# A second level of Strassen's scheme in the second FFN product, from the second chunk on

## The chip, the cores and the metric

The kernel runs on one core of one Trainium2 chip. The metric is the device time of one execution in microseconds, the median of several runs. Lower is better. The core's engines are TensorE (PE; PEld is its weight load), VectorE (DVE), ScalarE (ACT), GpSimd (POOL) and SyncE (SP, which here only starts DMAs). Each works through its own queue in order, and they wait for one another through semaphores.

## The reference

An attention block whose heads are mixed before and after the softmax feeds a Fourier mixing block with a feed-forward network (FFN). Only the end of it is touched by the change:

```python
    u = x + mixed
    mu = np.mean(u, axis=-1, keepdims=True)
    var = np.mean((u - mu) ** 2, axis=-1, keepdims=True)
    un = (u - mu) / np.sqrt(var + 1e-06)
    ch = np.maximum(un @ w_ch1, 0.0) @ w_ch2
    return (u + ch).astype(np.float32)
```

There are 8 x 448 = 3584 rows of 768 columns, and the hidden width is 3072. All is fp32; the weights arrive as 64-bit floats.

## The kernel before

The first 850 us or so are attention and Fourier mixing. The rest is the FFN, in `ffn_phase`. It cuts the rows into 7 blocks of 512 (`t`) and the hidden width into 6 chunks of 512 (`c`). One **step** `n` is one block times one chunk, 42 steps in all, blocks inside chunks. Each step makes two products, and each of these is done by one level of Strassen's scheme in its Winograd form: instead of eight products of half-size matrices, seven, with sums of the operands ahead and sums of the results behind.

`first(n)` makes the hidden values. Each of its seven parts (loop over `ORDER`) is six matmuls of 128 x 128 weights on 256 columns (L985). Parts accumulate into three PSUM tiles, called P, Q and R. ScalarE copies or VectorE adds what a part ends into the tile `h`, and ScalarE applies the ReLU. At the end VectorE makes the operand sums hs1, hs2 and h11 - h21 (L1020 to L1022).

`second(n, h)` multiplies them with the second weights. Each of its seven parts is four matmuls of 384 columns (L1042): two halves of the rows (`x`), and two blocks of the inner dimension (`kf`) that add up in PSUM. In chunk 0 VectorE adds the results to `u` and SyncE writes them out. In chunks 1 to 5 ScalarE copies them into `od` tiles, VectorE adds to these, and GpSimd starts a DMA that adds the tile to what is in memory (L1062). VectorE makes h12 - hs2 in the middle (L1065).

The weights of the next chunk are made ready alongside. `_Weights` turns the 64-bit numbers into 32-bit ones with seven VectorE instructions for each piece, forms the operand sums of the weights with four more for each slice, and writes them to scratch memory. A slice has four pieces, so 32 VectorE instructions; a chunk has five slices, three of the first weights (pieces 256 wide) and two of the second (384 wide). GpSimd starts the loads of the raw pieces (L213, two pieces ahead) and the writes (L221). `wts.add(c + 1, ...)` queues one slice in each of a chunk's early steps, and `wts.deal(k)` places up to `k` of the queued VectorE instructions at that point of the program: 3 after six of the seven parts of `first` and 4 after every part of `second`, 46 a step.

The order of TensorE's and VectorE's instructions in the FFN is the order of the program. ScalarE's and GpSimd's is left to the scheduler:

```python
    with tc.manual_schedule(engines={ET.PE, ET.DVE}):
```

[...]P, Q and R have two tiles each, and after the first step P and R share two more, so that every third request for P or R takes an extra tile.

## Time and profile before

| what | value |
|---|---|
| median of 3 runs | 2410.84 us (2409.32 to 2411.01) |
| the profiled execution | 2417.4 us, of which span 2415.6 us |
| granted TensorE clock | 0.994 of full speed |
| VectorE, 851 to 1158 us (chunk 0) | 213.73 of 307 us busy |
| VectorE, 1158 to 1195 us (a step with weight conversion) | 19.55 of 37 us busy |
| VectorE, 2152 to 2404 us (the last chunk, none) | 55.29 of 252 us busy |
| GpSimd in the same three | 62.25, 11.24, 32.73 us |
| output DMA, issue to landing | 6.3 us |
| raw weight load, issue to landing | 3.7 us |

A page line of a group gives the source line, the engine, the operation, what is written from what, the shapes and the number of instructions; then the busy time and the mean duration in ns; then the idle time ahead of them and what ended it. A timeline line gives start, length, engine, line, operation and, behind x, how many instructions of the kind were merged. An fp32 matmul shows as two instructions. Matmuls overlap in the pipeline, so one's duration is longer than the distance between two.

### The profile page before, as it was taken

The page shows a single profiled execution, that of the slowest core. Times are in us where ns is not written, and L with a number is a line of the kernel's source. Part 1 is how long each engine was busy: PE and PEld are TensorE (multiplying, and loading weights), DVE is VectorE, ACT ScalarE, POOL GpSimd, SP SyncE. Part 2 cuts the span into 40 slices and gives each one's busy share as a digit, 9 for nine tenths or more (in the row PEclk, how much of TensorE's full clock was granted, in tenths as well). Part 3 has the DMA queues.
Part 4 walks back from the last instruction along what each step waited for, and adds up shares of the span by engine and source line. Part 5 has one row for each costly group of instructions (what it writes and reads, how often), then busy time and mean ns, then how long its engine had stood idle before and what let it go on. Part 6 is the DMA issues. An engine that isn't in the chain of part 4 may idle for free.

```text
span 2415.6 us, 55276 instructions
## 1 busy us (share of the span) xinstructions
PE 2363.0 (98%) x21680; PEld 1592.6 (66%) x21680; DVE 1408.6 (58%) x2859; ACT 932.7 (39%) x2335; POOL 960.3 (40%) x1395
## 2 busy tenths in 40 slices
PE   6999999999999999999999999999999999999998
PEld 2555555555555577677777777777777777777775
DVE  3888888888887767775555255624552455421221
ACT  4777777666667532231222222222222222222221
POOL 3587877868776541210223023212222223111111
PEclk9999999999999999999999999999999999999999
DMA  7565555655554565658687677777686777585453
GB/s 160 163 179 167 183 172 166 190 162 180 169 164 157 165 248 184 213 180 308 165 198 187 182 201 171 197 184 201 173 205 149 221 190 188 137 232 112 108 115 53
DMA packets 207184, 427.59 MB, mean 177 GB/s; under 512 B 38990, under 2 KB 128870, under 8 KB 206926
## 3 DMA queue, kind: packets, MB, share of 16 engines
q1 hardware_dynamic: 129902, 261.60, 32.4%
q0 software_dynamic: 71456, 161.08, 31.1%
q8 instruction: 173, 2.83, 0.5%
q10 hardware_dynamic: 5568, 1.38, 0.4%
q14 instruction: 85, 0.70, 0.1%
HBM read 211.98 MB, written 129.39 MB: 141 GB/s over the span
## 4 chain that ended last, share of the span: by engine, by line
PE 77%; issue 11%; DMA 4%; DVE 2%; POOL 2%; ACT 1%; SPq 1%; POOLq 0%; ACTq 0%; DVEq 0%
PE psP L985 15%; PE psP L1042 14%; PE psR L985 7%; PE psR L1042 7%; PE mx L486 6%; PE ms L459 5%; PE ms L547 5%; PE po L520 5%; PE psQ L1042 4%; PE psQ L985 4%; DMA Kr<-Sb 3%; POOL out_dram L1062 2%; PE ms L661 2%; PE ms L434 1%; SPq L475 1%
## 5 line engine op out<-in xcount | busy, mean ns | idle before, releaser
L985 PE MATMUL psP<-ub,w1t 128*128 128x256 f32 x2016 | 462.5, 379 | 0.0
L1042 PE MATMUL psP<-w2t,h 128*128 128x384 f32 x1344 | 460.9, 486 | 0.0
L985 PEld LDWEIGHTS psP<-ub,w1t 128*128 128x128 f32 x2016 | 382.8, 190 | 60.7
L1062 POOL DMA_DIRECT2D out_dram<-od x140 | 170.9, 1221 | 590.5 <-DVE od L1060 467.7
L1042 PEld LDWEIGHTS psP<-w2t,h 128*128 128x128 f32 x1344 | 254.4, 190 | 165.9
L510 POOL TENSOR_SCALAR PP<-PP,rcp 128x448 f32<-128x448 f32 x384 | 253.8, 670 | 230.0 <-DVE rcp L508 201.2
L500 ACT ACTIVATE PP<-mx,nmx 128x448 f32<-128x448 f32 x384 | 240.7, 632 | 174.4 <-DVE nmx L493 162.9
L493 DVE TENSOR_REDUCE nmx<-mx 128x1 f32<-128x448 f32 x384 | 223.0, 617 | 94.4 <-PE mx L486 92.5
L213 POOL DMA_DIRECT2D raw<-in_moe_w_ch_dram x120 | 72.6, 605 | 515.1 <-DVE tmp L257 507.7
L1058 ACT COPY od<-psP 128x384 f32<-128x384 f32 x210 | 100.6, 479 | 437.1 <-PE psP L1042 437.1
L486 PE MATMUL mx<-Kr,kw 60*32 60x448 f32 x3072 | 236.4, 552 | 17.2 <-DMA Kr<-Sb 13.7
L996 DVE TENSOR_TENSOR h<-h,psQ 128x512 f32<-128x512 f32 x42 | 28.9, 687 | 381.3 <-PE psQ L985 381.3
L985 PE MATMUL psR<-ub,w1t 128*128 128x256 f32 x1008 | 231.3, 379 | 0.0
L1042 PE MATMUL psR<-w2t,h 128*128 128x384 f32 x672 | 230.5, 486 | 0.0
L531 DVE STREAM_TRANSPOSE Pv<-po 128x896 f32<-128x896 f32 x192 | 212.6, 1107 | 9.0 <-PE po L520 6.1
L520 PE MATMUL po<-PP,kw 60*32 60x448 f32 x3072 | 214.2, 543 | 3.4 <-POOL PP L510 1.8
L459 PE MATMUL ms<-kT,qT 64*32 64x448 f32 (+1 forms) x3072 | 207.2, 547 | 7.3 <-ACT qT L330 6.4
L985 PEld LDWEIGHTS psR<-ub,w1t 128*128 128x128 f32 x1008 | 191.4, 190 | 25.9
L330 ACT COPY Sb<-ms 124x448 f32<-124x448 f32 x384 | 184.0, 542 | 36.7 <-DMA Kr<-Sb 16.1
L547 PEld LDWEIGHTS ms<-Pv,vv 64*64 64x64 f32 x5376 | 144.5, 133 | 70.5 <-issue 37.3
L1042 PEld LDWEIGHTS psR<-w2t,h 128*128 128x128 f32 x672 | 127.2, 190 | 87.4
L547 PE MATMUL ms<-Pv,vv 64*64 64x120 f32 x5376 | 167.8, 269 | 1.0 <-issue 1.0
(101 smaller groups left out, 2925.0 us busy)
## 6 DMA issues: line engine op xcount, KB each, us to landing
ub<-ub SPq DMA_DIRECT2D x294, 384.0 KB
Kr<-Sb SPq DMA_DIRECT2D x768, 105.0 KB
out_dram<-od POOLq DMA_DIRECT2D x140, 384.0 KB, 6.3
raw<-in_moe_w_ch_dram POOLq DMA_DIRECT2D x72, 256.0 KB, 3.8
raw<-in_moe_w_ch_dram POOLq DMA_DIRECT2D x48, 384.0 KB, 3.7
w<-wst POOLq DMA_DIRECT2D x126, 128.0 KB, 3.5
w<-wst POOLq DMA_DIRECT2D x84, 192.0 KB, 3.5
w1t<-w SPq DMA_DIRECT2D x42, 384.0 KB
```

Of the source, the lines that this page charges most:

```text
L330: (nc.scalar.copy if eng == "a" else nc.vector.tensor_copy)(out=out, in_=in_)
L459: nc.tensor.matmul(pss[x][o:o + hi - lo, :S], st["qT", xx][64 * x:64 * x + 64, y, lo:hi], st["kT", xx][64 * x:64 * x + 64, y, :], start=Tr ...
L486: nc.tensor.matmul(mx[x][64 * z + o:64 * z + o + 32, :S], kw1[64 * x:64 * x + KR, o:o + 32], Kr[64 * x:64 * x + KR, z, :], start=True, sto ...
L493: nc.vector.tensor_reduce(nmx[:, :], steps[T]["mx"][x][:, :S], axis=AX.X, op=ALU.max, negate=True)
L500: nc.scalar.activation(steps[T]["PP"][:, x, :], steps[T]["mx"][x][:, :S], ACTF.Exp, bias=steps[T]["nmx", x][:, :], accum_out=steps[T]["den ...
L510: nc.gpsimd.tensor_scalar(PP[:, x, :], PP[:, x, :], rcp[:, x:x + 1], 1.0, op0=ALU.mult, op1=ALU.mult)
L520: nc.tensor.matmul(po[o:o + 32, z, :S], kw2[64 * z:64 * z + KR, y, :], PP[64 * z:64 * z + KR, :, c * HS:(c + 1) * HS], start=True, stop=True)
L531: nc.vector.transpose(g["Pv"][:, T % GT, :].rearrange("p (z s) -> p z s", z=2), steps[T]["po"][:, :, :S])
L547: nc.tensor.matmul(pss[y][64 * x:64 * x + 64, :nu * R], st["v", pr][64 * y:64 * y + 64, x, jb * D:(jb + 1) * D], _ap(Pv, 64 * y * rp + 32 ...
L985: nc.tensor.matmul(p[:, m, :], w1[i][:, kc, m * P:(m + 1) * P], ub[:, kc, :], start=i in OPENS and m == kc == 0, stop=kc == NK - 1, skip_g ...
L1042: nc.tensor.matmul(p, lhs[i][:, kf, x * P:(x + 1) * P], w2[i][:, kf, :], start=i in OPENS and kf == 0, stop=kf == FM - 1, skip_group_check ...
L1062: nc.gpsimd.dma_start(out=acc[t, r, d], in_=os[r, d][:, :, :], accum_op=ALU.add)
```

## The change

From chunk 1 on, each of the seven half-size products of the second product is made by the scheme once more. Its left operand is 256 rows by 256, its right one 256 by 384; so it becomes seven products of quarter size, each one matmul of 128 x 128 weights on 192 columns: 49 matmuls of 192 columns a step in place of 28 of 384.

The new operand sums are: `quarter`, four sums for each of the seven left operands, grouped (h11 and h22 on GpSimd, h21, hs1 and hs2 on VectorE, h12 and h12 - hs2 on GpSimd, 12 instructions in all a step); and `halves`, four sums for each of the seven right operands, on GpSimd, in the first step of each chunk (28 instructions). `second2` takes the results out of PSUM 192 columns at a time (`take` on ScalarE, `more` on VectorE) into seven whole tiles `od`, one for each half-size product, and `both` adds these up, four sums on VectorE and three on GpSimd. What does not depend on the second level keeps its place: four output DMAs a step, the loads of both weights, the loads of `ub`.

`second2` doesn't issue at once. It gives each action a slot; a half-size product starts every seven slots and its own actions reach over 20, so that neighbouring products interleave. Slots up to 48 are issued after `first` of the same step; slots 49 and later are issued among the matmuls of the next step's `first` (`SEAM` says ahead of which), and slot 0 goes ahead of the last two matmuls of its own `first`. The order of all four compute engines is now that of the program.

The weight conversion is dealt in `first` alone: 5, 5, 5, 5, 5, 2 and 0 after the seven parts, 27 a step. A slice is queued in each of the first five steps of a chunk, as before. In both products' chunk 0 the matmuls stay; VectorE's sums hs1, hs2 and h11 - h21 move ahead of the last part of `first`, and h12 - hs2 to its end.

```diff
+ORDER2 = (0, 3, 5, 6, 4, 1, 2)
...
-    pw2 = pool("pw2", 7)
+    pw2 = pool("pw2")
...
+    H11, H22, H21, HS1, HS2, H12, H12S = range(7)
+    LHS = (H11, H12, H12S, H22, HS1, HS2, H21)
+    def quarter(eng, hq, h, f0, f1, s):
+        o = hq[:, f0:f1, :, :]
+        a11, a12, a21, a22 = (h[:, f0:f1, f, x * P:(x + 1) * P]
+                              for x in range(2) for f in range(2))
+        to, a, b, op = ((o[:, :, 0], a21, a22, ALU.add),
+                        (o[:, :, 1], o[:, :, 0], a11, ALU.subtract),
+                        (o[:, :, 2], a11, a21, ALU.subtract),
+                        (o[:, :, 3], a12, o[:, :, 1], ALU.subtract))[s]
+        eng.tensor_tensor(to, a, b, op=op)
+    def halves(i):
+        wt[i] = right["wt"].tile([P, 3, DQ], F32, name="wt", tag=f"wt{i}")
+        b11, b12 = w2[i][:, 0, :DQ], w2[i][:, 0, DQ:]
+        b21, b22 = w2[i][:, 1, :DQ], w2[i][:, 1, DQ:]
+        t1, t2, t4 = (wt[i][:, x, :] for x in range(3))
+        for to, a, b in ((t1, b12, b11), (t2, b22, t1), (b12, b22, b12), (t4, b21, t2)):
+            nc.gpsimd.tensor_tensor(to, a, b, op=ALU.subtract)
+    def first(n, st, beside):
         c, t = divmod(n, NTB)
-        h = ph.tile([P, 6, FM, HT], F32, name="h", tag="h")
-        h11, h12, h22, h21, hs1, hs2 = (h[:, x] for x in range(6))
+        h = st["h"] = ph.tile([P, 7, FM, HT], F32, name="h", tag="h")
+        if c:
+            hq = st["hq"] = right["hq"].tile([P, 7, 4, P], F32, name="hq", tag="hq")
+        h11, h22, h21, hs1, hs2, h12, h12s = (h[:, x] for x in range(7))
         norms = c == 0 and t + 1 < NTB
+        vec = nc.vector
         ps = {}
+        done = 0
         for k, i in enumerate(ORDER):
+            if c and t == 0:
+                halves(ORDER2[k])
             if i in OPENS:
                 ps[ACC[i]] = ps_tile(ACC[i])
             p = ps[ACC[i]].rearrange("p (m t) -> p m t", m=FM)
             ub = ubs.pop((n, i))
             for m in range(FM):
                 for kc in range(NK):
+                    for fn in beside.pop(done, ()):
+                        fn()
+                    done += 1
                     nc.tensor.matmul(p[:, m, :], w1[i][:, kc, m * P:(m + 1) * P],
                                      ub[:, kc, :],
                                      start=i in OPENS and m == kc == 0,
@@ -993,13 +1025,16 @@
             elif i == 5:
                 nc.scalar.copy(out=h21, in_=p)
             elif i == 1:
-                nc.vector.tensor_tensor(h11, h11, p, op=ALU.add)
+                vec.tensor_tensor(h11, h11, p, op=ALU.add)
                 nc.scalar.activation(h11, h11, ACTF.Relu)
             elif i == 6:
-                nc.vector.tensor_tensor(h22, h22, p, op=ALU.add)
+                vec.tensor_tensor(h22, h22, p, op=ALU.add)
                 nc.scalar.activation(h22, h22, ACTF.Relu)
+                if c:
+                    for x in range(4):
+                        quarter(nc.gpsimd, hq, h, H11, H22 + 1, x)
             elif i == 2:
-                nc.vector.tensor_tensor(h21, h21, p, op=ALU.add)
+                vec.tensor_tensor(h21, h21, p, op=ALU.add)
                 nc.scalar.activation(h21, h21, ACTF.Relu)
             else:
                 nc.scalar.activation(h12, p, ACTF.Relu)
@@ -1009,26 +1044,34 @@
                     power(t + 1)
             if n == 0 and k not in (1, 2):
                 next_part()
-            if i != 2:
+            if c:
+                wts.deal((5, 5, 5, 5, 5, 2, 0)[k])
+            elif i != 2:
                 wts.deal(2 if norms else 3)
+            if i == 2:
+                vec.tensor_tensor(hs1, h21, h22, op=ALU.add)
+                vec.tensor_tensor(hs2, hs1, h11, op=ALU.subtract)
+                vec.tensor_tensor(h21, h11, h21, op=ALU.subtract)
+                if c:
+                    for x in range(4):
+                        quarter(vec, hq, h, H21, HS2 + 1, x)
             if t == NTB - 1 and c + 1 < NC:
                 load_w1(c + 1, i)
             if NTB <= n + 1 < NC * NTB:
                 new_ub(n + 1, i)
                 nc.sync.dma_start(out=ubs[n + 1, i][:, :, :],
                                   in_=ub_scr[(n + 1) % NTB][i])
-        nc.vector.tensor_tensor(hs1, h21, h22, op=ALU.add)
-        nc.vector.tensor_tensor(hs2, hs1, h11, op=ALU.subtract)
-        nc.vector.tensor_tensor(h21, h11, h21, op=ALU.subtract)
-        return h
-    def second(n, h):
+        vec.tensor_tensor(h12s, h12, hs2, op=ALU.subtract)
+        if c:
+            for x in range(4):
+                quarter(nc.gpsimd, hq, h, H12, H12S + 1, x)
+        assert not beside
...
+            if t == NTB - 1:
+                load_w2(1, i)
+    def second2(n, st):
+        c, t = divmod(n, NTB)
+        at = {}
+        D, ps = {}, {}
+        vec = nc.vector
+        def on(s, fn, *a):
+            at.setdefault(s, []).append(lambda: fn(*a))
+        def mm(j, m):
+            i = ORDER2[j]
+            h, hq = st["h"][:, LHS[i]], st["hq"][:, LHS[i]]
+            key = {0: "P", 5: "P", 6: "P", 3: "P", 4: "R", 2: "R", 1: "Q"}[m]
+            if m in (0, 4, 1):
+                ps[j, key] = ps_tile(key)
+            a = {0: h[:, 0, :P], 1: h[:, 1, :P], 3: h[:, 1, P:], 4: hq[:, 0], 5: hq[:, 1],
+                 6: hq[:, 2], 2: hq[:, 3]}[m]
+            b = {0: w2[i][:, 0, :DQ], 1: w2[i][:, 1, :DQ], 2: w2[i][:, 1, DQ:],
+                 3: wt[i][:, 2], 4: wt[i][:, 0], 5: wt[i][:, 1], 6: w2[i][:, 0, DQ:]}[m]
+            nc.tensor.matmul(ps[j, key][:, :DQ], a, b, start=m in (0, 4, 1), stop=True,
+                             skip_group_check=True)
+        def part(j, q):
+            if j not in D:
+                D[j] = right["od"].tile([P, 2, DH], F32, name="od", tag="od")
+            return D[j][:, q // 2, q % 2 * DQ:(q % 2 + 1) * DQ]
+        def take(j, q, key):
+            nc.scalar.copy(out=part(j, q), in_=ps[j, key][:, :DQ])
+        def more(j, q, key):
+            vec.tensor_tensor(part(j, q), part(j, q), ps[j, key][:, :DQ], op=ALU.add)
+        def both(eng, j, k):
+            eng.tensor_tensor(D[j][:, :, :], D[j][:, :, :], D[k][:, :, :], op=ALU.add)
+        def out_(j, r, d):
+            nc.gpsimd.dma_start(out=acc[t, r, d], in_=D[j][:, :, :], accum_op=ALU.add)
+        for j, i in enumerate(ORDER2):
+            b = 7 * j
+            for s, m, q, key in ((0, 0, 0, "P"), (3, 4, 3, "R"), (4, 5, 1, "P"),
+                                 (5, 1, None, None), (8, 6, None, None),
+                                 (13, 2, None, None), (16, 3, 2, "P")):
+                on(b + s, mm, j, m)
+                if key:
+                    on(b + s, take, j, q, key)
+            on(b + 8, more, j, 0, "Q")
+            on(b + 11, more, j, 3, "P")
+            on(b + 16, more, j, 1, "R")
             if t == NTB - 1 and c + 1 < NC:
-                load_w2(c + 1, i)
+                on(b + 17, load_w2, c + 1, i)
+        j0, j3, j5, j6, j4, j1, j2 = range(7)
+        pl = nc.gpsimd
+        for j, ops in ((j5, ((vec, j5, j0),)), (j6, ((vec, j6, j5), (pl, j3, j6))),
+                       (j4, ((pl, j6, j4), (pl, j5, j4))), (j1, ((vec, j0, j1),)),
+                       (j2, ((vec, j5, j2),))):
+            for o in ops:
+                on(7 * j + 19, both, *o)
+        on(7 * j6 + 25, out_, j3, 1, 0)
+        on(7 * j4 + 27, out_, j6, 1, 1)
+        on(7 * j1 + 23, out_, j0, 0, 0)
+        on(7 * j2 + 23, out_, j5, 0, 1)
+        return at
...
+        for n in range(NTB):
+            if 0 <= n - 1 < NK + FM:
+                wts.add(1, n - 1)
             wts.deal(0)
-            if c == 0 and t + 2 < NTB:
-                load_u(t + 2)
-            second(n, first(n))
+            if n + 2 < NTB:
+                load_u(n + 2)
+            st = {}
+            first(n, st, {})
+            second(n, st)
             wts.deal(1000)
             if n == 0:
                 assert not parts
                 rest.close()
-                pd.append(pool("pd", 6, side="right"))
+                for name, bufs in (("wt", 1), ("hq", 1), ("od", 7)):
+                    right[name] = pool("p" + name, bufs, side="right")
                 beside.close()
                 pps.append(pool("ppy", space=bass.MemoryType.PSUM))
+    SEAM = {49: 0, 50: 1, 51: 1, 52: 1, 53: 2, 54: 2, 55: 3, 56: 3, 57: 4, 58: 5, 59: 5}
+    with tc.manual_schedule(engines={ET.PE, ET.DVE, ET.Activation, ET.Pool}):
+        rest_ = {}
+        for n in range(NTB, NC * NTB):
+            c, t = divmod(n, NTB)
+            if c + 1 < NC and t < NK + FM:
+                wts.add(c + 1, t)
+            if t == NTB - 1:
+                wts.deal(1000)
+            st = {}
+            at = second2(n, st)
+            beside = {}
+            for s_ in sorted(rest_):
+                beside.setdefault(SEAM.get(s_, s_ - 54), []).extend(rest_[s_])
+            beside.setdefault(NK * FM * 7 - 2, []).extend(at.pop(0))
+            first(n, st, beside)
+            rest_ = {}
+            for s_ in sorted(at):
+                if s_ < 49:
+                    for fn in at[s_]:
+                        fn()
+                else:
+                    rest_[s_] = at[s_]
+        for s_ in sorted(rest_):
+            for fn in rest_[s_]:
+                fn()
```

## The prediction

> **What bounds the kernel now.** I read the page first, its busy times and groups, then the timeline of one step (one block of 512 rows times one sixth of the hidden width) in the second half, then the places where GpSimd and VectorE compute at the same moment.
>
> ```profile
> PE 2363.0 (98%) x21680; PEld 1592.6 (66%) x21680; DVE 1408.6 (58%) x2859; ACT 932.7 (39%) x2335; POOL 960.3 (40%) x1395
> ...
> L985 PE MATMUL psP<-ub,w1t 128*128 128x256 f32 x2016 | 462.5, 379 | 0.0
> L1042 PE MATMUL psP<-w2t,h 128*128 128x384 f32 x1344 | 460.9, 486 | 0.0
> ```
>
> TensorE is busy all the time, and both products have no idle time before them. The next lines, from the timeline, give the pitch, which the mean duration (pipelined) doesn't:
>
> ```profile
> 1502.08 2.75 PE L985 MATMUL psP<-ub,w1t 128*128 128x256 f32 x12
> ...
> 1520.21 2.74 PE L1042 MATMUL psP<-w2t,h 128*128 128x384 f32 x8
> ...
> 1538.27 2.75 PE L985 MATMUL psP<-ub,w1t 128*128 128x256 f32 x12
> ```
>
> Every fp32 matmul is two passes (12 for six matmuls). The first product takes 1520.21 - 1502.08 = 18.13 us for 84 passes, 216 ns each; the second 18.06 for 56, 322.5 ns each; a step is 36.19 us. Elsewhere, transposes 128 columns wide:
>
> ```profile
> 965.24 0.82 PE L952 MATMUL psQ<-ident,un 128*128 128x128 f32 x6
> ```
>
> Less the 273 ns of the last, five pitches take 0.55 us, 109 ns each. The three points lie on one line, 0.833 ns a column and 2.5 ns. So down to 128 columns no weight load shows, and a 192-column pass should take 162.5 ns, a matmul 325 ns.
>
> The change gives VectorE and GpSimd more work, so their overlap matters:
>
> ```profile
> 855.91 2.67 POOL L601 TENSOR_TENSOR xs<-X 113x384 f32<-113x384 f32 x2
> 856.25 6.08 DVE L964 TENSOR_TENSOR ub<-ub 128x768 f32<-128x768 f32 x4
> 858.66 1.59 POOL L606 TENSOR_TENSOR xs<-xs 113x383 f32<-113x383 f32 x1
> ...
> 862.86 2.94 POOL L622 TENSOR_TENSOR xf<-xq 113x385 f32<-113x385 f32 x3
> 863.42 0.50 DVE L672 TENSOR_TENSOR X<-X,ms 113x385 f32<-113x385 f32 x1
> ```
>
> L964 alone takes 0.95 us; here four take 6.08, 1.52 each, and L606 takes 1.59 where its median is 1.00. They run in turn. L672, one of whose inputs is PSUM, keeps its 0.50 under L622.
>
> **What the Trainium skill says.** "SBUF — State Buffer", section "Who interferes with whom": a VectorE instruction with two SBUF inputs, or in the mode that reads one tensor through both ports, contends with a GpSimd instruction that reads SBUF, and the first holds the ports for its whole length; PSUM operands avoid it. The lines above agree. "TensorE: Matmul & The Clock Gate", section "Back-to-back issue gap": columns over 2.4 GHz plus 2.5 ns; the three pitches agree.
>
> **The change, part by part.** It acts on 35 of the 42 steps (chunks 1 to 5).
>
> TensorE: 28 matmuls of 384 columns become 49 of 192. 49 x 0.325 = 15.93 us; with the first product 34.05 a step instead of 36.19. Gain 2.14 x 35 = 75 us. All else is at best hidden. In chunk 0 only VectorE's sums of h change place; VectorE was busy 214 of 307 us there, so nothing. The same DMAs are issued, SyncE's weight loads at the same points: nothing.
>
> Output of a step: 8 ScalarE copies and 6 VectorE adds, 384 wide, become 28 copies (0.32 us each, an estimate from 479 ns at 384 and 586 at 512) and 21 adds (0.35, from 554 ns at 384 and 688 at 512; pitch 0.3), 192 wide. ScalarE then has 13 of 34 us: hidden. The adds read PSUM, so they do not contend. The tail after the last matmul gains one full-width add (0.95) and loses half a copy: nothing.
>
> VectorE's other work in a step, in its written order: two sums of 768 (0.95), then the 27 weight-conversion instructions, now all in the first product, five after each of its first five parts, two after the sixth; three adds from PSUM (0.69, pitch 0.6); hs1, hs2, h21 (1.93 together by L1020 to L1022); four quarter sums 384 wide (2.1); h12s (0.6). A conversion costs 0.375 us where 256 wide (four at a pitch of 0.325, three of 0.455), 0.48 where 384 wide (0.39, 0.59). Only then come the first output adds, and the seventh half-size product of the first of seven (it accumulates in the same PSUM tile) waits for the second of these adds.
>
> GpSimd, by L601 (1.00 at 384) and L615 (0.59 at 192): a 256-wide quarter sum 0.73, eight of them; a 768-wide sum 1.8, three; and in the first step of a chunk 28 weight sums of 192, 0.57 each, 16 us, all inside the first product. No row shows a sum over the quarter sums' two strided pieces: 0.73 is the slope between those two rows, bounds 0.59 and 1.0; I take 0.73, because the step between pieces should cost little. Its order is now written too, so raw loads (0.55 us to issue, 3.7 to land) stand behind these sums, and VectorE's next conversion behind the load.
>
> Walk of an ordinary step, T = 0 at its first matmul. TensorE, with four left-over matmuls in the first part, ends parts at 3.9, 6.5, 9.1, 11.7, 14.3, 16.8 and 19.75 (one new matmul in the last). The waiting half-size matmul is due 11 x 0.325 later, at 23.3. GpSimd's two 768-wide sums run from about 1.0 to 4.5; VectorE's sum, ready at 1.6, shares the ports with them and VectorE is free for conversions at 5.75 instead of 3.2.
> - 256 wide: part 0's five to 7.65, second sum 8.6, ten more to 12.35, add 12.95, five to 14.85, add 15.45. ReLU lets GpSimd's quarter sums (2.9 us) start at 16.2, in turn with the next five conversions: done at 19.5, not 17.3. Add 20.2, ReLU 20.95, then 1.93 + 2.1 + 0.6 and two adds: 26.2. Late by 2.9.
> - 384 wide: 0.1 us more on 25 conversions, and the same sharing: late by 6.2 (6.0 where 25 are dealt).
> - Mixed (fourth step): 4.0.
> - No conversions (last step of a chunk, and chunk 5): add as soon as its part ends, 17.05, ReLU 18.4, the same tail with one GpSimd sum in front: late by 0.4 to 0.9; I take 0.7.
>
> First step of chunks 2 to 4: GpSimd does the two sums, four weight sums, two output writes (1.2 each), and only then the raw load, at 10.3; it lands at 14.0. VectorE converts from there: 16.95 after the first five and its sum. From then conversions, 20 more weight sums (11.4) and eight quarter sums share the ports: third add at 33.6, hs1 at 35.4, tail 44.7. Late by 21.4. In chunk 1 no left-over sums stand ahead: 6.9. In chunk 5, no conversions: 5.6.
>
> Late loads in steps two to five: the pair that opens a new weight slice is issued one deal before it is needed, 1.9 to 2.4 us against 4.3. Bounds 0 (idle VectorE covers) and 3; I take 0.8, since part lies in waits counted already.
>
> Sum of stalls: ten steps x 0.7 = 7; eight x 2.9 = 23; four x 4.0 = 16; four x 6.2 + four x 6.0 = 49; first steps 3 x 21.4 + 6.9 + 5.6 = 77; loads 16 x 0.8 = 13. Together 185, less 75: +110. The profiled execution took 2417.4 us (span 2415.6), 6.6 over the median of the runs, 2410.84; so about 2527 there and **2520** in the median.
>
> **Rivals.**
> 1. The ports are rarely wanted together in this stage, so VectorE and GpSimd keep their own durations. Then the walks give 0.4 late for steps without or with 256-wide conversions, 0.8 mixed, 1.4 for 384 wide, and 8.4 for the first steps of chunks 2 to 4 (GpSimd's order alone delays the load): 18 x 0.4 + 4 x 0.8 + 8 x 1.4 + 27 = 49. 2411 - 75 + 49 = 2385. For it: VectorE idles in the second product and can give way once. Against: the turns above, and GpSimd's sums fall just where VectorE converts.
> 2. Faster in full: TensorE stays the bound. Mechanism: the new order lets GpSimd and the loads run far enough ahead that the waiting matmul finds its add done, except the 0.4 us of the hs chain. 2411 - 75 + 14 = 2350. It decides if VectorE reaches the first output adds before T = 22.7, which needs the first step's weight sums done early. For it: chunk 1 has such a lead; against: the written order puts output writes and sums ahead in all others.
> 3. Weight loads show at 192 columns: 190 ns a pass (the PEld mean) instead of 162.5 makes the second product 18.6 us; the gain is gone, +19, plus rival 1's 49: about 2479. Against: 109 ns at 128 columns.
>
> **How the numbers follow.** Forecast 0.62, rival 1 0.20, rival 2 0.12, rival 3 0.06. The first-step bounds (10 to 25 late, three times), loads (0 to 3, sixteen times: -13 to +35) and half or all of the conversion lateness give the forecast's own range 2430 to 2590. Leaving out rival 2 and the ends, the whole range is 2380 to 2590. A measurement tells about 0.2%. Faster 0.31 (rivals 1, 2), same 0.03 (between the cases), slower 0.66.
>
> **What would show it.** Right: 192-wide passes at 162.5 ns, TensorE idle between the first product and the seventh half-size matmul, released by VectorE's output add; conversions and sums lengthened wherever GpSimd sums overlap; first steps near 55 us, steps without conversions near 34.8. Wrong: steps of 34 to 35 us everywhere, or VectorE's two-input sums at 0.95 under GpSimd's.

## The result, and the profile after

The changed kernel takes 2610.39 us, the median of four runs (2606.62 to 2614.8), beside 2410.08 us for the kernel before on the same chip: a ratio of 1.0834, 95% interval 1.0812 to 1.0856. It is slower by 200 us where the forecast had 110, and above its range. The profiled execution took 2608.26 us, span 2606.5.

From the page of the changed kernel: busy time of each engine, the granted TensorE clock in 40 slices, three groups and three rows of DMA issues (the last number is the time from issue to landing in us).

```profile
PE 2357.4 (90%) x23150; PEld 1813.2 (70%) x23150; DVE 1886.3 (72%) x3664; ACT 1102.7 (42%) x3035; POOL 1456.3 (56%) x1920
...
PEclk9999999999999999999999889988999899999999
...
L1017 PE MATMUL psP<-ub,w1t 128*128 128x256 f32 x2016 | 513.2, 395 | 132.5 <-DVE h L1031 132.5
...
L1140 POOL TENSOR_TENSOR od<-od 128x768 f32<-128x768 f32 x105 | 205.5, 2130 | 235.5 <-DVE od L1140 235.5
...
L1140 DVE TENSOR_TENSOR od<-od 128x768 f32<-128x768 f32 x140 | 249.6, 1783 | 35.4 <-ACT od L1134 33.8
...
raw<-in_moe_w_ch_dram POOLq DMA_DIRECT2D x72, 256.0 KB, 5.8
raw<-in_moe_w_ch_dram POOLq DMA_DIRECT2D x48, 384.0 KB, 7.2
w<-wst POOLq DMA_DIRECT2D x126, 128.0 KB, 7.4
```

TensorE is no longer the bound: 90% busy instead of 98%, and its largest idle time stands inside the first product (L1017), not in the second. The clock row, nines throughout before, now has eights in the second half. The sums L1140 take 1783 ns in the mean on VectorE, where they take 968 without GpSimd's (experiment 4). Raw loads land in 5.8 and 7.2 us instead of 3.8 and 3.7.

The lengths of the steps tell where the time goes. They are the distances between ScalarE's first copies of h in the timeline, in us, by chunk. Before, every step is 36.19.

| chunk | 1st | 2nd | 3rd | 4th | 5th | 6th | 7th |
|---|---|---|---|---|---|---|---|
| 1 | 42.7 | 46.5 | 44.7 | 41.7 | 40.0 | 40.5 | 34.9 |
| 2 | 57.5 | 46.5 | 43.2 | 41.6 | 40.5 | 41.9 | 34.9 |
| 3 | 58.4 | 47.0 | 43.9 | 42.2 | 38.8 | 40.5 | 34.9 |
| 4 | 60.0 | 46.3 | 43.5 | 41.5 | 40.5 | 41.6 | 34.9 |
| 5 | 42.1 | 34.9 | 34.9 | 34.9 | 34.9 | 34.9 | with the tail |
| prediction's walk | 41, 55.4, 39.7 | 37.75 | 37.75 | 38.85 | 41.05 | 40.05 | 34.75 |

(The walk's row is 34.05 plus the lateness it gives, with its 0.8 for late loads in steps two to five. Its three first steps are those of chunk 1, of 2 to 4, and of 5.)

The walk is near in the first, fifth, sixth and seventh steps. It misses the second by 8.8 us, the third by 6.1 and the fourth by 2.9. From the waits view of the changed kernel (1132 to 2600 us: engine, what it was about to write and at which line, for whom it waited; total us, times, longest):

```profile
PE psP L1017 <- DVE h L1031: 132.5, 23, 16.8
...
DVE tmp L235 <- DMA raw<-in_moe_w_ch_dram: 115.1, 19, 14.4
...
PE psP L1125 <- DVE od L1137: 36.9, 28, 5.1
...
POOL w L221 <- DMA out_dram<-od: 25.7, 15, 2.5
DVE wst L243 <- DMA w<-wst: 24.0, 8, 4.0
```

The wait that the prediction named, for VectorE's output add L1137, is only 37 us. TensorE loses 132 us earlier, at the last part of the first product: its PSUM tile of kind P is freed by VectorE's add L1031, which stands behind conversions in VectorE's order, and these wait 115 us for the raw loads. The second step of chunk 1 shows it, in timelines of GpSimd, VectorE and TensorE, put together in order of time:

```profile
1172.35 4.22 DVE L1140 TENSOR_TENSOR od<-od 128x768 f32<-128x768 f32 x1 [0.32 <-ACT od L1134]
...
1173.45 2.30 POOL L1140 TENSOR_TENSOR od<-od 128x768 f32<-128x768 f32 x1
...
1175.20 2.95 POOL L1143 DMA_DIRECT2D out_dram<-od  x2
1177.60 1.73 POOL L213 DMA_DIRECT2D raw<-in_moe_w_ch_dram  x2
...
1178.67 0.95 DVE L1140 TENSOR_TENSOR od<-od 128x768 f32<-128x768 f32 x1
...
1180.68 2.69 POOL L221 DMA_DIRECT2D w<-wst  x4
1185.43 0.55 POOL L221 DMA_DIRECT2D w<-wst  x1 [2.06 <-DMA out_dram<-od]
1186.46 0.29 DVE L235 TENSOR_SCALAR tmp<-raw 128x256 uint32<-128x256 uint32 x1 [6.83 <-DMA raw<-in_moe_w_ch_dram]
...
1193.40 0.29 DVE L243 TENSOR_SCALAR wst<-tmp 128x256 uint32<-128x256 uint32 x1 [3.63 <-DMA w<-wst]
1193.61 0.68 DVE L1028 TENSOR_TENSOR h<-h,psQ 128x512 f32<-128x512 f32 x1
...
1196.12 0.68 DVE L1031 TENSOR_TENSOR h<-h,psP 128x512 f32<-128x512 f32 x1
...
1196.86 3.78 PE L1017 MATMUL psP<-ub,w1t 128*128 128x256 f32 x8 [9.14 <-DVE h L1031]
...
1208.11 0.49 PE L1125 MATMUL psP<-w2t,h 128*128 128x192 f32 x2
1208.44 0.49 PE L1125 MATMUL psP<-w2t,hq 128*128 128x192 f32 x2
```

Read it from TensorE's wait backwards. It waits 9.14 us for L1031. VectorE reached that add late because it stood idle twice: 6.83 us until a raw piece landed, then 3.63 us until an earlier write of converted weights landed and freed its `wst` tile. The load was issued at 1177.60 and lands 8.9 us later, right behind two output writes in GpSimd's queue; the fifth weight write waits for an output write to land before it is issued at all.

The DMA records of this trace show what the load does in these 8.9 us. The two output writes issued at 1175.20 and 1176.87 are 256 packets of 1536 bytes each; the first ones run from 1177.48 to 1180.58, the second ones from 1181.05 to 1184.71. The first 4096-byte packet of the two raw pieces starts at 1183.42, and the last one ends at 1187.12. Meanwhile, from 1180 to 1182, over a hundred packets of SyncE's queue start. So the load waits its turn behind the writes in its own queue, while the DMA engines are full (share 1.03 in the window from 1174 to 1190 below).

The queue alone is not the whole cause, because the kernel before sends the same loads and writes through it. The views of line L213, the raw load, from 1132 to 2600 us end with these lines, before and after:

```profile
DMA to landing us min/median/max: 3.1/3.6/9.9
...
DMA to landing us min/median/max: 3.2/9.0/10.3
```

(The trace tells the landing of 21 of these loads before and of 26 after.) Before, 5 of the 21 were issued within 3 us after an output write and landed in 4.8 to 9.9 us, the other 16 in 3.1 to 5.7. After, 17 of the 26 were, and landed in 5.1 to 10.3 us, the other 9 in 3.2 to 7.9. What hid slow ones before was the lead: every load for chunks 2 to 5 was issued at least 15.9 us ahead of VectorE's first instruction on it, and VectorE never waited. In the changed kernel GpSimd's written order issues the load that opens a slice just ahead of its use, here 2.0 us before VectorE is free for it at 1179.62.

The line of TensorE has more: eight passes run from 1196.86 to the next matmul at 1200.43, 446 ns each instead of 216. The windows view of the same kernel (second column: length; then busy us of PE, PEld, DVE, ACT, POOL; granted clock; DMA share; GB/s) shows the clock at that point:

```profile
1174.00:1190.00 16.00, 13.72 (x65) 11.77 (x63) 8.60 (x17) 2.08 (x4) 10.46 (x13) 1.00 1.03 245
1190.00:1202.00 12.00, 5.14 (x13) 4.25 (x14) 8.25 (x18) 2.21 (x4) 4.42 (x6) 0.59 0.37 147
```

After this wait TensorE restarts at half clock. "TensorE: Matmul & The Clock Gate" in the Trainium skill, section "What's actually happening", says that an idle window of about 3.4 us halves the clock and as much activity restores it. This trace agrees: in chunks 1 to 5 its half-clock records last 3.4 us or a multiple of it, up to 17.1, and each of TensorE's 22 idle stretches of 3.2 us or more has one, of the 15 from 1.4 to 2.2 us only four. After the 13 of 4.7 us or more the record ends 3.0 to 5.8 us behind the restart. All of them together hold 184 us, before none. Of the passes begun there, 260 stand 1.5 to 2.4 times their normal pitch apart, 46 us more in all. Gaps between passes at any clock add 225 us. Together 271, less the 75 gained, are 196 of the 200 us measured. This says where TensorE's time went, not why.

### The profile page after: what moved, and what is told of

It is laid out like the page before. It is cut to its first block, busy times and chain, and to the rows that moved or that the text cites. A ratio compares the mean times of both kernels' runs of the same rounds, so it can differ in the third digit from the quotient of the medians.

```text
span 2606.5 us, 60515 instructions
## 1 busy us (share of the span) xinstructions
PE 2357.4 (90%) x23150; PEld 1813.2 (70%) x23150; DVE 1886.3 (72%) x3664; ACT 1102.7 (42%) x3035; POOL 1456.3 (56%) x1920
## 4 chain that ended last, share of the span: by engine, by line
PE 58%; DVE 15%; DMA 11%; issue 7%; POOL 6%; ACT 1%; SPq 1%; ACTq 0%; POOLq 0%; DVEq 0%
PE psP L1125 9%; PE psP L1017 8%; PE mx L486 6%; PE ms L459 5%; PE ms L547 5%; PE po L520 5%; PE psR L1125 4%; DMA w<-wst 4%; PE psR L1017 3%; DMA raw<-in_moe_w_ch_dram 3%; PE psP L1085 3%; DMA Kr<-Sb 2%; PE psQ L1125 2%; POOL od L1140 2%; DVE od L1140 2%
## 5 line engine op out<-in xcount | busy, mean ns | idle before, releaser
L1017 PE MATMUL psP<-ub,w1t 128*128 128x256 f32 x2016 | 513.2, 395 | 132.5 <-DVE h L1031 132.5
L1017 PEld LDWEIGHTS psP<-ub,w1t 128*128 128x128 f32 x2016 | 393.6, 199 | 190.7 <-DVE h L1031 141.9
L1134 ACT COPY od<-psP 128x192 f32<-128x192 f32 x735 | 234.8, 319 | 381.5 <-PE psP L1125 379.3
L1140 POOL TENSOR_TENSOR od<-od 128x768 f32<-128x768 f32 x105 | 205.5, 2130 | 235.5 <-DVE od L1140 235.5
L1140 DVE TENSOR_TENSOR od<-od 128x768 f32<-128x768 f32 x140 | 249.6, 1783 | 35.4 <-ACT od L1134 33.8
L983 POOL TENSOR_TENSOR hq<-h 128x256 f32<-128x256 f32 x140 | 110.8, 792 | 283.1 <-ACT h L1032 155.7
L1017 PE MATMUL psR<-ub,w1t 128*128 128x256 f32 x1008 | 231.3, 379 | 0.0
L1143 POOL DMA_DIRECT2D out_dram<-od x140 | 186.7, 1358 | 62.8 <-DVE od L1140 44.5
L1017 PEld LDWEIGHTS psR<-ub,w1t 128*128 128x128 f32 x1008 | 191.4, 190 | 25.9
L221 POOL DMA_DIRECT2D w<-wst x210 | 123.2, 644 | 89.2 <-DVE wst L261 39.0
L1137 DVE TENSOR_TENSOR od<-od,psQ 128x192 f32<-128x192 f32 x245 | 85.9, 351 | 116.4 <-ACT od L1134 97.1
L213 POOL DMA_DIRECT2D raw<-in_moe_w_ch_dram x120 | 84.4, 792 | 139.6 <-DVE tmp L257 122.2
```

Of the source, the lines that this page charges most:

```text
L1017: nc.tensor.matmul(p[:, m, :], w1[i][:, kc, m * P:(m + 1) * P], ub[:, kc, :], start=i in OPENS and m == kc == 0, stop=kc == NK - 1, skip_g ...
L1134: nc.scalar.copy(out=part(j, q), in_=ps[j, key][:, :DQ])
L1140: eng.tensor_tensor(D[j][:, :, :], D[j][:, :, :], D[k][:, :, :], op=ALU.add)
```

## The experiments

Theory A: the loads and weight writes that share GpSimd's queue with the output writes are late, and VectorE's conversions hand that on to TensorE. Theory B: the sums of the second level (GpSimd's and VectorE's sharing the ports, and the weight sums of a chunk's first step) are the main cost. Theory C: the conversion, now dealt in the first product alone, is too dense whatever feeds it. (The recorded expectations name their theories anew for each run; their letters are not these.)

**1. No conversion.** From chunk 1 on no slice is queued, and chunks 2 to 5 use chunk 1's weights.

```diff
-            if c + 1 < NC and t < NK + FM:
-                wts.add(c + 1, t)
...
-        nc.sync.dma_start(out=w1[i][:, :, :], in_=wts.w1[c][i])
+        nc.sync.dma_start(out=w1[i][:, :, :], in_=wts.w1[min(c, 1)][i])
```

> From chunk 1 on no weight is converted and none of the raw loads and weight writes is issued; chunks 2 to 5 compute with the weights of chunk 1. Theory A (the stalls come from the conversions on VectorE, late because their loads are late and because they share ports with GpSimd): the second to sixth step of every chunk takes the 34.9 us that steps without conversions take now, the first steps of chunks 2 to 4 the 42 us that chunk 5's takes; 2610 - 155 - 50 = about 2405 us. Theory B (GpSimd's own sums and their order stall TensorE whatever VectorE converts): steps two to six stay at 40 to 46 us, and the time stays above 2520.

2402.64 us. Steps two to seven all last 34.9, the first ones 37.4 to 42.1. So with all of the second level in place 208 us come from the conversion beside it. Without any conversion the kernel is only 0.3% faster than before (ratio 0.9971, interval 0.9955 to 0.9986), so the stalls of the second level itself use up nearly all of the 75 us gained. It leaves A and C open.

**2. Weight sums in chunk 1 only.** The later chunks' sums are left out; they use those of chunk 1.

```diff
-            if c and t == 0:
+            if c == 1 and t == 0:
```

> GpSimd's 28 weight sums are made in chunk 1 only; chunks 2 to 5 use those of chunk 1 (and the unsummed second weights), so 112 GpSimd instructions of 0.6 us are left out. Theory A (late loads and shared ports): the first steps of chunks 2 to 4 fall from 58 to 60 us to what the second steps take, about 45, chunk 5's from 42 to 35; other steps stay as they are; about 2610 - 3 x 14 - 7 = 2560 us. Theory B (the weight sums throw GpSimd back so far that the second and third steps suffer too): second steps fall from 46.5 to below 42 as well, and the time below 2530.

2573.99 us, 36 less than the changed kernel. The first steps of chunks 2 to 4 fall from 57.5 to 60.0 to 45.9 to 48.0, chunk 5's to 34.9. Second steps stay at 46.6: the sums explain the first steps alone.

**3. Raw loads on SyncE** (from the second converted chunk on), the rest as it was.

```diff
-                nc.gpsimd.dma_start(out=raw[:, :f, :].rearrange("p f w -> p (f w)"),
+                (nc.sync if k >= 40 else nc.gpsimd).dma_start(out=raw[:, :f, :].rearrange("p f w -> p (f w)"),
```

> The raw weight loads of chunks 2 to 5 are started by SyncE on its own queue; nothing is left out. Theory A (they are late because they stand behind the 384 KB output writes in GpSimd's queue): they land in about 4 us in place of 6 to 9, VectorE's idle time at the first conversion instruction (119 us in all) goes below 30, second steps fall from 46.5 to 39 to 40, third from 44 to 39, first ones by 5; about 2610 - 85 = 2525 us. Theory C (they are late because all 16 DMA engines are busy, or the ports hold VectorE anyway): landing stays above 6 us or the steps stay within 2 us of now; above 2580.

2549.53 us, 61 less but 25 more than expected. VectorE's wait for the raw pieces is gone from the waits view; a new one stands near the top:

```profile
DVE wst L243 <- DMA w<-wst: 73.9, 12, 7.7
...
PE psP L1017 <- DVE h L1031: 65.9, 19, 6.5
```

The second steps last 43.2 to 43.9 (42.9 in chunk 1). The weight writes, still in GpSimd's queue, took the loads' place as the next late thing: 24 us of waiting became 74.

**4. GpSimd's three result sums left out** (the output is then incomplete).

```diff
-        for j, ops in ((j5, ((vec, j5, j0),)), (j6, ((vec, j6, j5), (pl, j3, j6))),
-                       (j4, ((pl, j6, j4), (pl, j5, j4))), (j1, ((vec, j0, j1),)),
+        for j, ops in ((j5, ((vec, j5, j0),)), (j6, ((vec, j6, j5),)),
+                       (j1, ((vec, j0, j1),)),
```

> GpSimd's three sums of 768 a step are left out (three of the four quarters of the output are incomplete). Theory A (shared ports): VectorE's sums of 768 go from a mean of 1.78 us to about 1.0, VectorE is free 2.6 us earlier in each step, fifth and sixth steps fall from 40 to 41.6 us to 37.5 to 39; steps without conversions stay at 34.9 because they have that slack; about 2610 - 24 x 2.6 = 2548 us. Theory D (the ports matter little and only late DMAs do): fifth and sixth steps stay within 0.7 us of now, above 2595.

2492.43 us: it saves 118 where I had expected about half. The group of VectorE's sums on its page:

```profile
L1140 DVE TENSOR_TENSOR od<-od 128x768 f32<-128x768 f32 x140 | 135.5, 968 | 46.0 <-ACT od L1134 45.9
```

Alone the sums take 968 ns, beside GpSimd's 1783: 114 us of VectorE's time. Without the sums GpSimd also comes to its writes and loads earlier; the wait for raw pieces falls from 115 to 71 us. Second steps last 41, later ones 36.3 to 39.8. So B's shared ports and A are two pieces of one chain, and part of this saving is A's.

**5. Raw loads and weight writes on SyncE.** The edit of experiment 3, and

```diff
-            self.later.append(lambda: nc.gpsimd.dma_start(out=dst[slot], in_=box[slot]))
+            self.later.append(lambda: (nc.sync if c >= 2 else nc.gpsimd).dma_start(
+                out=dst[slot], in_=box[slot]))
```

> As the run with the raw loads on SyncE, and the writes of the converted weights of chunks 2 to 5 too; nothing is left out. Theory A2 (there the late weight write took the place of the late load: the single buffer that VectorE writes next comes free only when the write before it has landed, and that stands behind the output writes in GpSimd's queue): VectorE's wait at L243 goes from 74 us to below 15, second and third steps from 43 to 38 to 39; about 2549 - 30 = 2519 us. Theory C (the DMA engines are full, any queue is slow): second and third steps stay above 42, the time above 2540.

2499.34 us, 111 less than the changed kernel. From its waits view:

```profile
PE psP L1126 <- DVE od L1138: 48.6, 32, 4.0
...
PE psP L1018 <- DVE h L1032: 30.3, 19, 4.3
DVE wst L244 <- DMA w<-wst: 26.8, 12, 4.1
```

TensorE's wait inside the first product falls from 132 to 30 us, and the one the prediction named, for VectorE's output add, is now the longest. The wait for the weight writes falls from 74 us (experiment 3) to 27, not below 15 as expected. Second steps last 37.6 to 38.1, thirds 39.1 to 40.0, fourths 37.9 to 39.1, fifths 38.7 to 39.0, sixths 39.0 to 39.8: the walk's row within 2.4 us. First steps of chunks 2 to 4 last 47.7, less than the walk's, which had their loads late. The passes' gaps fall from 225 to 136 us and the slow clock's extra from 46 to 23. Theory A holds for what the prediction missed, and the rival of the recorded text, that the DMA engines are full and any queue is slow, had 2540 us or more. Of the 111 us, 78 come from steps two to six and 33 from the first steps of chunks 2 to 4.

The trace says how it helps. The pieces that VectorE takes up at 1178.62 and 1181.60, in the second step of chunk 1, were issued by SyncE at 1131.07 and 1143.79, 48 and 38 us ahead; every load for chunks 2 to 5 is issued 8.8 us or more ahead, and VectorE waits for none. A load on SyncE isn't quicker by itself: the next one, issued at 1181.83 while the DMA engines are full (share 1.0 to 1.2 from 1181 to 1189), ends its last packet at 1188.95, 7.1 us later. What is gained is that the issue no longer waits behind GpSimd's sums and output writes.

**6. Conversion spread**: of the 27 instructions of a step, 17 are dealt in the first product and ten among the second product's slots.

```diff
-                wts.deal((5, 5, 5, 5, 5, 2, 0)[k])
+                wts.deal((4, 4, 3, 3, 3, 0, 0)[k])
...
+        for s in (18, 21, 24, 27, 30, 34, 36, 39, 42, 45):
+            on(s, wts.deal, 1)
```

> The 27 conversion instructions of a step are dealt 4, 4, 3, 3, 3, 0, 0 in the first product and ten in the second, where VectorE idles; nothing is left out. Theory A (VectorE is late at the seam because all conversions stand ahead of its first output adds): ten fewer at 0.375 to 0.48 take 4 to 5 us from VectorE's way there; fifth and sixth steps fall from 40.5 to 36 to 37, fourth to 37.5; second and third still wait for loads, 42 and 40; about 2610 - 75 = 2535 us. Theory E (VectorE has no room in the second product either, its adds come late there): no step gains more than 1 us, above 2590.

2532.18 us. Fifth and sixth steps fall from 40 and 41 to 35.8 and 36.5 in the mean, second and third stay at 43.6 to 48.1. C is right about the later steps, where the loads come in time, and not about the second and third.

**7. Two of GpSimd's sums on VectorE.**

```diff
-                       (j4, ((pl, j6, j4), (pl, j5, j4))), (j1, ((vec, j0, j1),)),
+                       (j4, ((vec, j6, j4), (vec, j5, j4))), (j1, ((vec, j0, j1),)),
```

> The two sums of 768 that GpSimd makes at the seam are made by VectorE; the third stays; nothing is left out. Theory A (a GpSimd sum costs VectorE more through the shared ports than it would cost VectorE to make it): VectorE pays 2 x 0.95 = 1.9 us and is spared 3.6 us of waiting, and GpSimd's output writes and loads go out 3.6 us earlier; steps fall by 1.5 to 3 us, about 2610 - 50 = 2560 us; with the sums left out altogether it was 2492, of which the two late ones are most. Theory F (what counts is VectorE's own work): steps with conversions rise by 1 to 2 us, above 2620.

2563.66 us, 47 less. VectorE makes half as many sums again in less time (210 sums at a mean of 972 ns against 140 at 1783), because it no longer stands still under two GpSimd sums issued back to back.

**8. All four**: experiments 5 and 7, a spread like 6 (4, 4, 4, 3, 3 in the first product, 2 after each of the first five parts in a chunk's first step), and the weight sums moved away from where conversions run.

> All three edits together, and of the weight sums of chunks 2 to 5 three of seven moved into the last step of the chunk before, the other four behind the quarter sums that TensorE needs first; the first step of a chunk deals 20 conversions, the others 28. Nothing is left out. Theory A: steps with conversions 35 to 36.5 us, first steps 36 to 39, the rest 34.9; 2410 - 45 + 24 x 1 + 4 x 2 = 2385 to 2410 us, as fast as before or a little faster. If other stalls take over, single steps stay above 38.

2406.33 us, a ratio to before of 0.9995, interval 0.9984 to 1.0005: no difference. Second to sixth steps with conversion last 34.9 to 36.2 us, seventh ones 36.4 to 37.1, first ones 37.4 to 39.1. TensorE waits 40 us for the output adds. Experiments 5, 6 and 7 alone saved 111, 78 and 47 us, 236 in all; together, with the weight sums moved as well, they save 204. So the savings overlap.

**9. All, and later sums.** Experiment 8 with the last two of VectorE's quarter sums, h12 - hs2, and GpSimd's quarter sums of h12 put behind the first output adds (slot 12), and the weight sums' places adjusted to it.

```diff
-                    for x in range(4):
+                    for x in range(2):
                         quarter(vec, hq, h, H21, HS2 + 1, x)
...
+        def late():
+            if c:
+                for x in range(2, 4):
+                    quarter(vec, hq, h, H21, HS2 + 1, x)
+            vec.tensor_tensor(h12s, h12, hs2, op=ALU.subtract)
+            if c:
+                for x in range(4):
+                    quarter(nc.gpsimd, hq, h, H12, H12S + 1, x)
...
+        on(12, lambda: st["late"]())
```

> As the run of all four edits, with two more. VectorE makes two of its four quarter sums and h12 - hs2 after its first output adds, not ahead of them, and GpSimd's quarter sums of h12 follow there; the weight sums of the last two half-size products, needed latest, go into the second product of the first step, and only one product's are made in the last step of the chunk before. Nothing is left out. Theory A (what is left in every step is VectorE's chain of sums ahead of the first output adds, 1.6 us of which are not due yet): steps without conversions from 34.9 to 34.1, with conversions 34.2 to 35, first and last steps of a chunk below 36; 35 steps at 34.5 instead of 36.19 are 59 us, about 2350 us. If the sums moved only make later products late, steps stay at 34.9 and more, 2390 or above.

2369.59 us, ratio 0.9834, interval 0.982 to 0.9847: 1.7% faster than the kernel before. Steps without conversion last 34.2, near the floor of 34.05.

**10. The later sums alone**, on the changed kernel.

> The changed kernel with the one edit that VectorE's last two quarter sums and h12 - hs2, and GpSimd's quarter sums of h12, follow the first output adds. Nothing is left out. Theory A: ten steps without conversions go from 34.9 to 34.1; those with conversions lose 1 to 2 us of their stall; about 2610 - 35 x 1.2 = 2568 us. Otherwise (the stall at the seam has another cause than this chain): 34.9 stays.

2565.26 us, as expected. Its seventh steps fall to 34.2 as in 9. The second steps stay at 44.4 to 46.9 behind their loads.

**11. Loads first in the same queue.** The first two pieces of a new slice are loaded when it is queued, ahead of the left-over output writes, by GpSimd as before.

```diff
+        if c >= 2 and n < 3:
+            load(k0 + self.ahead - 1)
```

> The first two raw pieces of a new slice are loaded where the slice is queued, ahead of the left-over output writes and GpSimd sums of the step before, but still by GpSimd's queue; in the first three steps of chunks 1 to 4. Nothing is left out. Theory (the loads are late because they stand behind those writes and sums in GpSimd's order): VectorE's wait for the raw pieces, 119 us in the changed kernel, falls under 60 us, the second steps shorten from 46.5 to about 43.5 us and the first ones by 8 to 10 us, as they did with SyncE issuing the loads; in all about 2560 us. Rival (it is the kind of queue, or the engines that move the data, whatever the order): the raw pieces still take over 6 us to land, the second steps stay at 46 us, and the time stays over 2595 us.

2600.55 us. First steps of chunks 2 to 4 shorten to 52.3 to 52.5, by 5 to 8 us, as order would have it; second steps get longer, 47.4 to 48.2. Its waits:

```profile
DVE wst L243 <- DMA w<-wst: 88.2, 12, 12.0
...
POOL raw L213 <- DMA out_dram<-od: 39.1, 16, 3.8
...
DVE tmp L235 <- DMA raw<-in_moe_w_ch_dram: 36.3, 16, 4.0
```

VectorE's wait for the raw pieces fell from 115 to 36 us as expected, but the wait for the weight writes rose from 24 to 88, and GpSimd now stands 39 us (12 in the changed kernel) before later loads until output writes have landed. So the wait named by the theory fell, but the second steps and the total are the rival's (over 2595 us), and the 10 us saved are hardly more than the runs scatter. It isn't enough to be ahead of the writes once: the weight writes, and the later loads, still take their turn in GpSimd's order and queue.

**12. Fewer conversions in the second product**: experiment 9 with the deal 5, 4, 4, 4, 3 (3, 3, 3, 2, 2 in first steps) and eight slots in place of ten.

```diff
-                wts.deal(((4, 4, 4, 3, 3, 0, 0) if t else (2, 2, 2, 2, 2, 0, 0))[k])
+                wts.deal(((5, 4, 4, 4, 3, 0, 0) if t else (3, 3, 3, 2, 2, 0, 0))[k])
...
-        for s in (18, 21, 24, 27, 30, 34, 36, 39, 42, 45):
+        for s in (19, 22, 25, 28, 31, 35, 37, 43):
```

> The combined version with the late sums moved, with the conversion dealt 5, 4, 4, 4, 3, 0, 0 in the first product (3, 3, 3, 2, 2 in a chunk's first step) and eight instead of ten among the second product's slots. Nothing is left out. Theory (the 0.8 to 1.1 us that fourth to sixth steps last over the 34.2 us of a step without conversion come from conversions that delay the output adds in the second product): these steps fall to 34.5 to 35 us, 8 to 12 us in all, about 2360 us. Rival (the first product has no room for two more): the time stays within 3 us of 2370 or rises.

2359.34 us, ratio 0.978, interval 0.9751 to 0.981: the best, some 55 us below the kernel before. Two lines of its page:

```profile
PE 2297.5 (97%) x23150; PEld 1773.4 (75%) x23150; DVE 1817.4 (77%) x3734; ACT 1101.7 (47%) x3035; POOL 1213.0 (51%) x1630
...
PEclk8999999999999999999999999999999999999999
```

TensorE is 97% busy and the clock whole again. Steps last 34.2 to 35.1, first ones 36.2 to 36.8 (34.7 in chunk 5). No half-clock time is left in chunks 1 to 5.

## Why the prediction was partly right and its size wrong

Right, with numbers:
- **The gain.** 192-wide matmuls stand 325 ns apart (1208.11 and 1208.44 in the timeline above; the 24th after the first starts at 1215.91), as taken from the line through three widths. The floor of 34.05 is nearly reached, 34.2, in experiments 9 and 12. Rival 3, weight loads that show, is out: it had 190 ns a pass, and these are 162.5.
- **Steps without conversion.** 34.75 forecast, 34.9 measured; experiment 10 takes 0.7 of it by moving the named sums behind the adds.
- **The shared ports.** VectorE's first sum was to end at T + 5.75; the timeline has 1172.35 + 4.22, and the step's first matmul started at 1170.71: T + 5.9. The second was to end at 8.6; it ends at 1178.67 + 0.95, T + 8.9. Rival 1, in which each engine keeps its duration, falls with experiment 4. "SBUF — State Buffer", section "Who interferes with whom", in the Trainium skill says that the first of two such instructions holds the ports for its whole length. The 4.2 us here are more than one GpSimd sum of 1.8 accounts for: two of them, issued one behind the other, stand beside it, and the sum ends 0.82 us after the second.
- **First steps** of chunks 2 to 4: 55.4 forecast, 57.5 to 60.0 measured; of chunks 1 and 5, 41 and 39.7 against 42.7 and 42.1. The order of events in chunk 2's is the one forecast: the raw load is issued 9.5 us after the step's first matmul (forecast 10.3). It lands at 18.1, though, not at 14.0: 8.6 us after issue (L213 at 1428.52, L235 at 1437.12, first matmul at 1419.05). The mistake named below is in these steps too.
- **Fifth and sixth steps**: 41.05 and 40.05 against 40.0 and 41.1 in the mean. With the loads in time (experiment 5) they last 38.7 to 39.8, so the walk was a little long here and part of the agreement is luck.

Wrong: **the term "Late loads in steps two to five ... Bounds 0 and 3; I take 0.8"**, 13 us in the sum. The lead of about 2 us was right (2.0 in the second step of chunk 1). But it priced the load by before's landing time, 3.7 us, though the new order issues it right behind output writes and it lands 8.9 us later, and it left out the weight writes in the same queue, whose landing VectorE also waits for. The two waits there are 6.83 and 3.63 us, above the bound of 3 as well. Taking both kinds of transfer out of GpSimd's order (experiment 5) saves 78 us in steps two to six, where the term had 13. The excess over the walk says about the same. Mean excess over the walk, four times each: second steps 8.8, third 6.1, fourth 2.9, sixth 1.1, less 1.1 in the fifth. That is 71 us, on top of the 13. With 13.8 in the first steps (9.6 in chunks 2 to 4, 4.2 in the others) and 0.15 in each of ten steps without conversion it makes 86 of the 90 us by which the forecast was short. Experiment 5 brings the steps back to the walk's numbers.

Two terms stood at nothing. One is TensorE's restart at half clock: by the count of passes above about 1.6 us in each second step and 4.6 in each first step of chunks 2 to 4, 46 us in all. It follows from the waits and shrinks with them; it lies in the lengths counted already, and no run separates it from them. The other is the tail after the last matmul. From the start of the last matmul it takes 14.5 us where before took 9.1, mostly because VectorE's sum shares the ports there too (10.6 in experiment 4, 11.1 in experiment 7):

```profile
2591.64 4.01 POOL L1140 TENSOR_TENSOR od<-od 128x768 f32<-128x768 f32 x2
...
2591.96 4.52 DVE L1140 TENSOR_TENSOR od<-od 128x768 f32<-128x768 f32 x1 [0.32 <-ACT od L1134]
```

With these 5.4 us the account comes to 92 us for the 90 that were short.

Rival 2's condition, VectorE at the output adds in time, was the right one to name: experiments 9 and 12 nearly meet it, by moving five things (loads and weight writes, conversions, result sums, weight sums, late sums); TensorE still waits 17 and 10 us for these adds there, and they come to 2370 and 2359 where that rival had 2350. The change as made does not meet it.

"DMA: Bandwidth & Descriptors" in the Trainium skill, section "Issuing engines are not separate DMA queues", says that issuing from several engines saves only the time to start the transfers. The landings agree: 7.1 us for the load on SyncE, 8.9 for the one on GpSimd. But the start was what came late here, behind GpSimd's other work, and it was worth 111 us.

What stays open: how much of a landing of 8.9 us is the turn in the queue and how much the DMA engines that are busy while output writes run. It is also open how much of the 111 us is the 0.6 to 0.8 us of GpSimd's own time that each of these issues takes. No run separates them.

## What to carry to other kernels

Price a transfer by what stands ahead of it in the new order, on the engine that issues it and in its queue, not by its median landing in the old one. Look at the lead, from issue to use, in both orders. Follow each buffer that a transfer frees as well as each that it fills. When a change fills the slack of two engines that share ports and of the queue they feed, expect savings that overlap: here single remedies gave 10 to 111 us each, and only all together turned a loss of 8.3% into a gain of 2.2%. Put what the next matmul waits for ahead of work that nobody waits for, in each engine's written order, before judging the arithmetic saved.

## What had not been expected of the hardware

- TensorE's restarts at half clock: passes 446 ns apart instead of 216 after a wait of 9.14 us; 184 us of half clock in chunks 1 to 5, from waits of 2 to 17 us, and none in these chunks before.
- A VectorE sum of two operands in SBUF, 0.97 us alone, lasted 4.1 to 5.4 us once in each of 35 steps, where two GpSimd sums of 1.8 us alone followed one another.
- In the kernel before, a raw load of 256 or 384 KB landed in 3.1 to 5.7 us, but in 4.8 to 9.9 when it was issued within 3 us after an accumulating output write of 384 KB in the same queue. On SyncE's queue, with the DMA engines full, one took 7.1.
- Output writes that accumulate land in 7.8 us (6.3 before), and GpSimd's later DMA issues waited up to 3.2 us (3.8 in experiment 11) for them to land before they started.
